# In the first of four batches the chunk of 384 tokens is worked first instead of last

## The chip, the cores and the metric

The kernel runs on one core of a Trainium2 chip. The metric is the device time of one execution in microseconds (us), as a median over executions. The profile is of one execution; its span, from the first to the last instruction, is about 2 us shorter than the device time.

Names used below: TensorE (PE, with its weight loads PEld), VectorE (DVE), ScalarE (ACT), GpSimd (POOL) and SyncE (SP). PSUM is the memory that TensorE writes its products to. A **chunk** is a run of up to 4 tiles of 128 tokens; exT holds the exponentials of the softmax. The **chain** of a page is the work that ended last, followed back from the last instruction to the first; the **granted clock** is the share of full speed that TensorE was given.

## The reference, cut to what matters

```
def _attn_ref(q, k, v, tau):                    # 4 batches, 6016 tokens, 256 channels
    qn = q / (norm(q, axis=1) + 1e-06)
    kn = k / (norm(k, axis=1) + 1e-06)
    s = kn.transpose(0, 2, 1) @ qn / tau        # 256 x 256 for each batch
    ...                                         # softmax of s, row by row: a
    return v @ a
def _moe_ref(x, w_gate, w_val, w_out):          # x: 24064 x 256, weights 256 x 1536
    g = x @ w_gate
    return (silu(g) * (x @ w_val)) @ w_out
```

The kernel multiplies the 256 x 256 softmax into w_gate and w_val for each batch, so the tokens of v go straight through two products with these folded weights (Wg, Wv) and one with w_out. 6016 tokens are 47 tiles: eleven chunks of 4 tiles and an odd one of 3. Since q and k are summed over all tokens and v is handled token by token, the order of v's chunks is free.

## The kernel before

```
chunks = [(s, min(CS, NS - s)) for s in range(0, NS, CS)]     # CS = 4, NS = 47: the 3 come last
...
def load_first_v():
    nc.gpsimd.dma_start(
        out=v0_sb, in_=v[0, :CS * P, :].rearrange("(p s) c -> p s c", s=CS))

def transpose_first_v():                # TensorE, not a transfer: 8 transposes
    vt_ps = psum_o.tile([P, CH, CS * P], BF16, tag="o")
    for h in range(CH):
        for j in range(CS):
            nc.tensor.transpose(vt_ps[:, h, j * P:(j + 1) * P],
                                v0_sb[:, j, h * P:(h + 1) * P], ident)
    ...
def evacuate_first_v(h):
    nc.vector.tensor_copy(vt_ready[(0, 0)][:, h, :], state["vt_ps"][:, h, :])
...
def first_softmax(b):                   # end of the start of batch 0
    ...
    row_eps(rs)
    transpose_first_v()
    keep_warm(2)                        # two products whose result nobody reads
    for h in range(CH):
        evacuate_first_v(h)
    ...                                 # exp -> exT; row sums; first folded weights
    for u in range(4):
        wp_evacuate(b, u, units[u], lo, u % 2 == 1)
    nc.scalar.preload_act_table(ACT.Silu)
...
def gv_matmuls(b, ci, f, between=None): # one of 12 steps f of a chunk
    ...
    for dst, W in ((g_ps, Wg), (v_ps, Wv)):
        if between is not None and dst is v_ps:
            between()                   # in the first chunk: a unit of folded weights
        for kk in range(CH):
            nc.tensor.matmul(dst[:, :mv], W[:, kk, fs], vT[:, kk, :mv],
                             start=(kk == 0), stop=(kk == CH - 1))
...
plan[S1 + 20].append((norm_spread,))    # row of k's norms to all partitions: the tile ink
S2 = S1 + (28 if b == 1 else 34)
plan[S2].append((logits, 0))            # VectorE reads ink, eight steps later
```

Loads go out in the order k, q, v of the first chunk (v0), then the weights, with v of the second chunk among them. Steps 2 to 5 (counted from 0) of the first chunk also compute the other folded weights, whose evacuation out of PSUM alternates between VectorE and ScalarE. The last three lines prepare the next batch while the current one is worked.

## Time and profile before

| | before |
|---|---|
| device time at first, 3 executions | 810.24 us (809.68 to 813.17) |
| span of the profiled execution | 807.6 us |
| TensorE busy | 787.9 us, 98% |
| first value product / second chunk starts | 37.85 / 51.80 us |
| ScalarE's table load | 37.71, for 1.28 us |

To read it: the first 28 us of the chain are loads (of k and q), and nearly all of the rest is TensorE's own work. Around the last softmax step of that start, TensorE, ScalarE, VectorE and the loads hand work to each other within tenths of a microsecond. The lines are in the prediction.

### The profile page before, as it was taken

How to read it: one execution, taken by the hardware profiler on the slowest of the kernel's cores; microseconds unless marked ns; L12 is line 12 of the kernel's file. 1: busy time of each engine (PE TensorE's matmuls, PEld its weight loads, DVE VectorE, ACT ScalarE, POOL GpSimd, SP SyncE). 2: the span in 40 equal slices, each digit the busy share in tenths (PEclk: the TensorE clock that was granted, in tenths of full speed). 3: DMA queues.
4: the chain of work that ended last, by engine and by line, in shares of the span. 5: the costliest groups of instructions: out<-in, count | busy, mean ns of one | idle time of the engine just before them, and what ended most of it. 6: DMA issues, size and time to landing. Idle time of an engine off the chain costs nothing.

```text
span 807.6 us, 11833 instructions
## 1 busy us (share of the span) xinstructions
PE 787.9 (98%) x3867; PEld 384.4 (48%) x3940; DVE 554.7 (69%) x854; ACT 454.3 (56%) x802; POOL 251.0 (31%) x302
## 2 busy tenths in 40 slices
PE   4999999999999999999999999999999999999998
PEld 3644444444454444444454444444445444444446
DVE  4777878758667878766766778766866665665654
ACT  4666666555556666555555656555555555555553
POOL 4415887332104786332000777610000000000000
PEclk8999999999999999999999999999999999999999
DMA  9995999799886685887976697667556665565443
GB/s 89 143 154 97 147 190 174 144 142 178 149 145 144 131 153 121 152 137 166 145 170 144 113 160 149 131 126 166 128 116 123 144 134 131 125 149 130 117 113 99
DMA packets 203567, 112.43 MB, mean 139 GB/s; under 512 B 151424, under 2 KB 190337, under 8 KB 202753
## 3 DMA queue, kind: packets, MB, share of 16 engines
q1 hardware_dynamic: 185456, 84.55, 44.1%
q0 software_dynamic: 17904, 27.01, 30.6%
q8 instruction: 31, 0.51, 0.3%
q14 instruction: 32, 0.25, 0.1%
q10 hardware_dynamic: 144, 0.10, 0.0%
HBM read 79.06 MB, written 60.48 MB: 173 GB/s over the span
## 4 chain that ended last, share of the span: by engine, by line
PE 95%; DMA 3%; issue 1%; ACT 0%; DVE 0%; POOL 0%; ACTq 0%; POOLq 0%
PE g_ps L458 30%; PE v_ps L458 30%; PE o_new L499 29%; PE ps L425 2%; DMA q_sb<-in_q_dram 2%; PE kq_new L171 2%; PE o_new L552 1%; DMA k_sb<-in_k_dram 1%; ACT silu L464 0%; DVE sv L468 0%; PE ss_new L198 0%; PE last_ps L576 0%; PE unit_ps L425 0%; PE kq_new L176 0%; PE ps L415 0%
## 5 line engine op out<-in xcount | busy, mean ns | idle before, releaser
L468 DVE TENSOR_TENSOR sv<-silu,v_ps 128x512 bf16<-128x512 bf16 (+1 forms) x576 | 386.5, 673 | 214.5 <-ACT silu L464 213.1
L464 ACT ACTIVATE silu<-g_ps 128x512 bf16<-128x512 f32 (+1 forms) x576 | 339.1, 589 | 292.5 <-PE g_ps L458 263.7
L458 PE MATMUL g_ps<-vT,Wg 128*128 128x512 bf16 (+1 forms) x1109 | 326.5, 375 | 1.2
L458 PE MATMUL v_ps<-vT,Wv 128*128 128x512 bf16 (+1 forms) x1104 | 325.1, 374 | 1.0
L499 PE MATMUL o_new<-sv,w_out_sb 128*128 128x512 bf16 (+1 forms) x1079 | 319.1, 375 | 1.4
L458 PEld LDWEIGHTS <-Wv 128*128 128x128 bf16 x1152 | 112.7, 98 | 130.9 <-ACT Wv L437 0.4
L303 POOL TENSOR_TENSOR acc_new<-acc_new,sq 128x512 f32<-128x512 f32 x135 | 157.2, 1165 | 52.6 <-DVE sq L293 37.3
L458 PEld LDWEIGHTS <-Wg 128*128 128x128 bf16 x1152 | 111.3, 98 | 125.8 <-DVE Wv L435 0.2
L499 PEld LDWEIGHTS <-w_out_sb 128*128 128x128 bf16 x1104 | 108.0, 98 | 126.5
L129 POOL DMA_DIRECT2D vb_new<-in_v_dram x47 | 24.2, 516 | 244.9 <-DMA vT<-vb_new 243.8
L509 DVE COPY pl<-o_new 128x512 uint16<-128x512 uint16 (+1 forms) x92 | 62.5, 680 | 14.1 <-ACT pl L508 13.9
L293 DVE TENSOR_TENSOR sq<-q_sb 128x512 bf16<-128x512 fp8e5 x72 | 65.8, 914 | 0.0
L508 ACT COPY pl<-o_new 128x512 uint16<-128x512 uint16 (+1 forms) x92 | 53.1, 578 | 19.8 <-PE o_new L499 19.1
L294 ACT ACTIVATE sq<-k_sb 128x512 bf16<-128x512 fp8e5 x72 | 44.2, 614 | 0.0
L171 PE MATMUL kq_new<-k_sb,q_sb 128*128 128x512 fp8e5 x184 | 28.4, 295 | 1.4 <-DMA q_sb<-in_q_dram 1.3
L114 POOL DMA_DIRECT2D q_sb<-in_q_dram x45 | 25.4, 564 | 11.7 <-DMA k_sb<-in_k_dram 9.8
L198 PE MATMUL ss_new<-sq,ones_bf 128*128 128x256 bf16 x83 | 14.8, 336 | 10.9 <-ACT sq L188 10.9
L171 PEld LDWEIGHTS <-q_sb 128*128 128x256 fp8e5 x184 | 21.2, 137 | 6.3 <-DMA q_sb<-in_q_dram 2.7
L114 POOL DMA_DIRECT2D k_sb<-in_k_dram x42 | 23.2, 554 | 2.9 <-DVE sv L468 1.7
L370 POOL TENSOR_SCALAR den<-th 128x512 f32<-128x512 f32 x3 | 1.8, 614 | 64.4 <-ACT th L369 64.4
L338 POOL TENSOR_TENSOR inv<-inv,half 64x8 f32<-64x8 f32 x3 | 5.0, 1665 | 53.3 <-DVE inv L336 53.3
L298 POOL TENSOR_TENSOR acc_new<-sq 128x512 f32<-128x512 bf16 x3 | 3.5, 1151 | 47.1 <-DVE sq L293 47.1
(90 smaller groups left out, 208.4 us busy)
## 6 DMA issues: line engine op xcount, KB each, us to landing
rows<-pl SPq DMA_DIRECT2D x86, 256.0 KB, 2.6
out_dram<-ot_new SPq DMA_DIRECT2D x43, 512.0 KB, 4.1
vb_new<-in_v_dram POOLq DMA_DIRECT2D x43, 256.0 KB, 4.8
q_sb<-in_q_dram POOLq DMA_DIRECT2D x36, 128.0 KB, 5.9
k_sb<-in_k_dram POOLq DMA_DIRECT2D x33, 128.0 KB, 7.4
ot_new<-rows SPq DMA_TRANSPOSE x92, 3.7
k_sb<-in_k_dram POOLq DMA_DIRECT2D x5, 256.0 KB, 9.0
rows<-pl SPq DMA_DIRECT2D x6, 192.0 KB, 2.4
```

The source lines that it names most:

```text
L114: nc.gpsimd.dma_start(out=dst[:, gs:gs + gm, :], in_=src[b].rearrange("(p s) c -> p s c", s=NS)[:, gs:gs + gm, :])
L129: nc.gpsimd.dma_start(out=vb[:mv, :].rearrange("(p s) c -> p (s c)", s=cm), in_=v[b, cs * P:cs * P + mv, :].rearrange("(p s) c -> p (s c)" ...
L171: nc.tensor.matmul(kq[:, jh, :], q_sb[:, ps:ps + 2, js], k_sb[:, ps:ps + 2, :], start=(t == 0 and jh == 0), stop=last, perf_mode=DR, skip_ ...
L293: nc.vector.tensor_mul(sq[:, :pm, 0, :], q_sb[:, ps:ps + pm, :], q_sb[:, ps:ps + pm, :])
L294: nc.scalar.activation(sq[:, :pm, 1, :], k_sb[:, ps:ps + pm, :], ACT.Square)
L303: nc.gpsimd.tensor_tensor(out=acc, in0=acc, in1=sq[:, s, :, :], op=ALU.add)
L458: nc.tensor.matmul(dst[:, :mv], W[:, kk, fs], vT[:, kk, :mv], start=(kk == 0), stop=(kk == CH - 1))
L464: nc.scalar.activation(silu[:, :mv], g_ps[:, :mv], ACT.Silu)
L468: nc.vector.tensor_mul(sv[:, f, :mv], silu[:, :mv], v_ps[:, :mv])
L499: nc.tensor.matmul(self.o_ps[h][:, :self.mv], w_out_sb[:, f, h * P:(h + 1) * P], self.sv[:, f, :self.mv], start=(f == 0), stop=(f == FH - 1))
L508: nc.scalar.copy(pl[:, 0, :self.mv], halves[:, 0, :self.mv])
L509: nc.vector.tensor_copy(pl[:, 1, :self.mv], halves[:, 1, :self.mv])
```

## The change

The intent is plain from the diff: the first chunk's v is the only one that is loaded directly and transposed on TensorE ahead of the first product; three tiles in place of four make that stretch shorter. The odd chunk of batch 0 moves to the front for it.

```diff
-    chunks = [(s, min(CS, NS - s)) for s in range(0, NS, CS)]
-    NCH = len(chunks)
+    odd = NS % CS
+    assert odd
+    plain = [(s, min(CS, NS - s)) for s in range(0, NS, CS)]
+    chunks = [[(0, odd)] + [(s, CS) for s in range(odd, NS, CS)]] + [plain] * (B - 1)
+    NCH = len(plain)
...
-    v0_sb = const.tile([P, CS, C], BF16)
+    v0_sb = const.tile([P, odd, C], BF16)
...
-            out=v0_sb, in_=v[0, :CS * P, :].rearrange("(p s) c -> p s c", s=CS))
+            out=v0_sb, in_=v[0, :odd * P, :].rearrange("(p s) c -> p s c", s=odd))
...
-            for j in range(CS):
+            for j in range(odd):
...
-        nc.vector.tensor_copy(vt_ready[(0, 0)][:, h, :], state["vt_ps"][:, h, :])
+        nc.vector.tensor_copy(vt_ready[(0, 0)][:, h, :odd * P],
+                              state["vt_ps"][:, h, :odd * P])
...   (elsewhere chunks[ci] becomes chunks[b][ci])
```

More of the change, by code (lines that the diff above doesn't have):

```diff
@@ L124, in load_v @@
     def load_v(b, ci):
-        cs, cm = chunks[ci]
+        cs, cm = chunks[b][ci]
         mv = cm * P
@@ L134, in transpose_v @@
     def transpose_v(b, ci):
-        mv = chunks[ci][1] * P
+        mv = chunks[b][ci][1] * P
         vb = vb_loaded.pop((b, ci))
@@ L446, in gv_matmuls @@
     def gv_matmuls(b, ci, f, between=None):
-        cs, cm = chunks[ci]
+        cs, cm = chunks[b][ci]
         mv = cm * P
@@ L470, in out_rows @@
     def out_rows(b, ci):
-        cs, cm = chunks[ci]
+        cs, cm = chunks[b][ci]
         pat = "(p s) c -> p s c" if (b, ci) == (0, 0) else "(s p) c -> p s c"
@@ L483, in __init__ @@
         def __init__(self, b, ci, sv):
-            self.cm = chunks[ci][1]
+            self.cm = chunks[b][ci][1]
             self.mv = self.cm * P
@@ L533, in __init__ @@
         def __init__(self, b, ci, sv):
-            self.cm = chunks[ci][1]
+            self.cm = chunks[b][ci][1]
             self.sv = sv
```

## The prediction

> **What bounds the kernel now.** I read the page's busy times and chain first, to see which engine ends the run.
>
> ```profile
> PE 787.9 (98%) x3867; PEld 384.4 (48%) x3940; DVE 554.7 (69%) x854; ACT 454.3 (56%) x802; POOL 251.0 (31%) x302
> ...
> PE 95%; DMA 3%; issue 1%; ACT 0%; DVE 0%; POOL 0%; ACTq 0%; POOLq 0%
> ```
>
> TensorE is busy 98% of 807.6 us and is 95% of the chain; transfers are 3%, all at the start (loads of k and q, to about 28 us in the chain by time). So a saving counts only if it removes TensorE work or TensorE idle time, or shortens the start. Next I read the timeline of the start, 23 to 52 us, where every edited line runs.
>
> ```profile
> 23.74 0.53 POOL L143 DMA_DIRECT2D v_sb<-in_v_dram  x1 [1.99 <-DMA q_sb<-in_q_dram]
> ...
> 34.93 0.62 PE L150 MATMUL vt_ps<-ident,v_sb 128*128 128x128 bf16 x8
> ...
> 35.33 0.91 ACT L261 ACTIVATE exT<-s_f,inq 128x256 bf16<-128x256 f32 x2 [0.44 <-DVE inq L247]
> ...
> 35.59 0.76 DVE L157 COPY vT_new<-vt_ps 128x512 bf16<-128x512 bf16 x2
> ...
> 35.89 0.11 PEld L267 LDWEIGHTS <-exT 128*128 128x128 bf16 x2 [0.41 <-ACT exT L261]
> ...
> 37.71 1.28 ACT L285 ACT_TABLE_LOAD   x1
> ...
> 39.00 1.08 ACT L464 ACTIVATE silu<-g_ps 128x512 bf16<-128x512 f32 x2
> ...
> 39.65 0.59 PE L458 MATMUL g_ps<-vT_new,Wg 128*128 128x512 bf16 x2
> ...
> 40.15 0.59 PE L425 MATMUL ps<-w_gate_sb,exT 128*128 128x512 bf16 x2
> ...
> 51.80 0.59 PE L458 MATMUL g_ps<-vT,Wg 128*128 128x512 bf16 x2
> ```
>
> The reader is to see four things. The softmax result exT, not v, releases TensorE at 35.89. ScalarE cannot do the first silu before its table load ends at 39.00. The third gate product (39.65) starts about when that first silu ends. The second chunk starts at 51.80. Last I read the transfer views of single issues, for when the data behind v0 arrive (time from issue to landing is the last number).
>
> ```profile
> v_sb<-in_v_dram POOLq DMA_DIRECT2D x1, 256.0 KB, 11.1
> ...
> w_gate_sb<-in_moe_w_gate_dram POOLq DMA_DIRECT2D x1, 256.0 KB, 6.6
> ...
> vT<-vb_new SPq DMA_TRANSPOSE x1, 10.7
> ...
> w_out_sb<-in_moe_w_out_dram POOLq DMA_DIRECT2D x1, 768.0 KB, 14.1
> ```
>
> Issued at 23.74, 33.53, 38.85 and 36.56, they land at about 34.8 (v0), 40.1 (second gate weight piece, used at 40.15), 49.6 (the second chunk's transposed v, used at 51.80) and 50.7 (w_out, first used at 52.67). The margins of the last two are about 2 us each; the first two are just in time.
>
> **What the Trainium skill says.** "TensorE: Matmul & The Clock Gate", section "Back-to-back issue gap", gives a warm gap of N/2.4 + 2.5 ns for one isolated matmul: 215.8 ns at N=512, 162.5 at N=384, and a shorter sustained figure at 512. The trace agrees with the formula: products of 512 columns start 0.216 us apart, and those of 384 at the end 0.163 (two start at 787.08, the next two at 787.41). So 384 tokens cost three quarters; there is no fixed cost to win. "ScalarE: Activation LUTs", section "What ACT_TABLE_LOAD costs", measures 1283 ns and a drain of 1380; the trace has the 1.28 us, and the silu follows at once, with no drain after it. "DMA: Bandwidth & Descriptors", section "Issuing engines are not separate DMA queues", says that all transfers interleave on the same 16 engines. The trace agrees: w_out takes 14.1 us beside the second chunk's transposing transfer.
>
> **Part by part.**
>
> *What is only moved.* Batch 0 has 47 tiles in either order. A chunk of 384 saves 12 x 4 x (0.2158 - 0.163) = 2.5 us of gate and value products, and 24 x 0.053 = 1.3 us of output products, against one of 512. Those 3.8 us now fall in the first two chunks' time and return at the end of batch 0, where a full chunk takes the place of the short one. Balance: zero, if TensorE is saturated at both ends. It is at the old end: around 222 to 246 us the trace has products at 0.216 and 0.163 without gaps, across the boundary of batches too.
>
> *What is removed.* Two of the 8 TensorE transposes go. The 8 take 0.62 us less the pipeline of one (starts from 34.93 to the warming product at 35.39), so some 0.06 each: 0.12 us. But TensorE then waits for exT at 35.89 anyway; the warming products end their issue near 35.82. Worth on the path: 0. The two VectorE copies shrink from 0.76 to about 0.6 us; VectorE then idles 0.24 us for the row sums (36.59) today, so again 0. v0's source shrinks from 512 to 384 KB. The 1 MB loads of k and q each take 2.42 us (issues released at 9.24, 11.70, 14.22, 16.64), so 128 KB is about 0.3 us (an estimate from that rate): everything queued behind v0 lands 0.3 us earlier. The start is q-bound and v0 is behind q, so the start itself does not move, except perhaps 0.07 us where the value weights come just in time (a gap at 36.25).
>
> *What is lost in the first chunk.* The first gate product still starts near 37.4. In the old order TensorE then has g, v (0.86), four short weight products (0.43), g, v (0.86): it reaches the third gate product at 39.6, and the silu that frees its PSUM buffer ends there: a stall of some 0.06. Now it has 0.65 + 0.43 + 0.65 = 1.73 and is there at 39.15. The silu cannot start before 39.00 (the table load is unmoved) and takes about 0.49 at 384 columns (the row at 788.69 shows 0.49), so TensorE starts at about 39.55. New stall 0.4, old 0.06: of the 0.43 saved so far, only 0.1 is kept; **lost: 0.33 us**, or 0.25 if the start gains its 0.07.
>
> *The rest of the chunk.* Four steps with two weight units each cost 4 x 0.163 + 4 x 0.216 = 1.52 us. VectorE has 0.55 + 0.75 = 1.30 in them, ScalarE 0.49 + 0.69 = 1.18, so TensorE still sets the pace; the weight pieces land 0.3 us earlier and TensorE is 0.1 to 0.9 us earlier in them, tight but enough. Six plain steps cost 0.65 each, against ScalarE 0.49 and VectorE 0.55. From 39.55: + 4 x 1.52 + 6 x 0.65 gives 49.5 for the second chunk, 2.3 us before today's 51.80.
>
> *Arrivals there.* The second chunk's v, at 49.6 today, should be there by 49.3 to 49.5; w_out, needed 0.86 us into that chunk at 50.4, lands at about 50.4. Both margins of 2 us are spent almost exactly. I charge **0.1 us** for the two.
>
> *Sum.* 0 (moved work) + 0 (removed) + 0.3 (silu behind the table load) + 0.1 (arrivals) = **+0.4 us**, so 810.24 + 0.4, about 810.6 us.
>
> **The rivals.** (1) *The change pays at the start.* If the transposes waited for v0's landing (34.8, against 34.93 for the first of them), a landing 0.3 us earlier plus 0.12 of transposes would start everything behind it sooner, to 809.8. For it: those two times lie within 0.1 us. Against: TensorE had other work (L389) up to that moment, and the next release is exT at 35.89, which comes from q through ScalarE and not from v0. (2) *The second chunk's v or w_out comes late.* Both transfers are in a stretch where the 16 engines are full to about 48 us, with a sparse tail after. If that tail does not move with v0's 0.3 us, or TensorE gets there sooner than I work out, the stall is 0.3 to 1 us: 811 to 811.5. For it: TensorE needs them 2.3 us sooner and they gain at most 0.3. Against: today's margins are 2 us. (3) *VectorE becomes the bound of the first chunk*, through the two output buffers that its weight evacuations free: 1.30 of 1.52 us a step, worth 0.1 to 0.2 us at the first of them only. (4) *Later background work* (loads of batch 1, norms on GpSimd) runs against a TensorE that is 3.8 us ahead; its steps are counted in chunks, not time, and its margins are many microseconds: 0.
>
> **Range and chances.** My sum has a spread from -0.4 (rival 1) to +1.2 (rival 2), and the three runs before spread from 809.68 to 813.17. So 809.5 to 812.0 should hold it 8 times in 10. Two per cent is 16 us; nothing edited touches more than 5 us of work, and that work is conserved. Faster by 2%: 0.005; within: 0.985; slower: 0.01.
>
> **What would show each step.** Right: exT still released at about 35.9 with 6 transposes ahead of it; the table load still at 37.7; the third gate product at about 39.5 with an idle of some 0.4 us before it; the second chunk's first product between 49.4 and 49.8; products of 512 columns at the end of batch 0; and a total that is flat. Step wrong: if exT comes before 35.8, the start was bound by v0; if the third gate product starts by 39.2, the silu did not hold it; if the second chunk starts after 50, rival 2 holds. The prediction as a whole is wrong if the time falls below 809.5, which needs a saving that I found no place for, or rises over 812, which needs a stall of over 1 us.

## The result, and the profile after

| | before | after |
|---|---|---|
| median of 6 executions | 810.33 us | 810.69 us |
| all six, in order | 809.68, 810.24, 810.29, 810.37, 810.52, 813.17 | 809.90, 810.10, 810.43, 810.95, 811.95, 814.13 |
| ratio of the means | | 1.0007, 95% interval 0.9984 to 1.0029: the same |
| span of the profiled execution | 807.6 us | 812.4 us |

The ratio is the mean time of one kernel's runs over that of the other's of the same rounds, so not quite the ratio of the two medians. Before any line is read, one thing has to be seen: the profiled execution of the changed kernel is the slowest of its six (814.13), and that of before is a quick one (809.42, taken apart from its six and below all of them). **The 4.8 us between the two spans are not the effect of the change**, whose medians differ by 0.36. The work of reading is to find out which parts of the 4.8 belong to the change.

From the page after, busy times and the chain's shares by engine:

```profile
PE 794.6 (98%) x3938; PEld 385.4 (47%) x3938; DVE 554.5 (68%) x854; ACT 454.0 (56%) x802; POOL 250.9 (31%) x302
...
PE 92%; DMA 6%; POOL 1%; issue 0%; DVE 0%; ACT 0%; SPq 0%; POOLq 0%; DVEq 0%; ACTq 0%
```

TensorE still sets the end. The larger busy time is not more work: it is partly matmul records that were missing before (3867 against 3938, though the program has two products fewer), partly slow products. New is that transfers hold 6% of the chain and not 3%.

**The start.** The timeline after; columns are start, length, engine, line, what, count, and in brackets the idle time before and who ended it.

```profile
32.41 0.65 PE L176 MATMUL kq_new<-k_sb,q_sb 128*128 128x512 fp8e5 x4 [1.20 <-DMA q_sb<-in_q_dram]
...
37.06 0.82 PE L154 MATMUL vt_ps<-ident,v_sb 128*128 128x128 bf16 x6
...
37.92 0.62 DVE L161 COPY vT_new<-vt_ps 128x384 bf16<-128x384 bf16 x2 [0.59 <-PE vt_ps L154]
...
38.10 0.15 PEld L272 LDWEIGHTS <-exT 128*128 128x128 bf16 x1 [0.28 <-ACT exT L266]
...
40.65 1.28 ACT L290 ACT_TABLE_LOAD   x1
...
41.63 0.49 PE L463 MATMUL v_ps<-vT_new,Wv 128*128 128x384 bf16 x2
...
41.95 0.49 ACT L469 ACTIVATE silu<-g_ps 128x384 bf16<-128x384 f32 x1
...
43.04 0.49 PE L463 MATMUL g_ps<-vT_new,Wg 128*128 128x384 bf16 x2
```

The matching product of q and k ran at 30.98 before; here its q came late and it ran at 32.41, 1.4 us later, after an idle TensorE. That load was issued at 14.22 in both executions and landed after 18.2 us in place of 16.7. Then the distance grows: the first value product is at 41.63 and not at 37.85, 3.8 us later. The two lines before:

```profile
30.98 0.68 PE L171 MATMUL kq_new<-k_sb,q_sb 128*128 128x512 fp8e5 x4
...
37.85 0.59 PE L458 MATMUL v_ps<-vT_new,Wv 128*128 128x512 bf16 x2
```

The stretches of the trace say why; columns are the stretch, its length, busy time and count for PE, PEld, DVE, ACT and POOL, then the granted TensorE clock, the share of the transfer engines and GB/s. Before:

```profile
33.00:34.00 1.00, 1.00 (x16) 0.74 (x15) 0.70 (x2) 0.98 (x2) 0.96 (x2) 1.00 1.15 194
```

The clock is the third number from the end of the line, here 1.00. After:

```profile
31.00:32.00 1.00, 0.22 (x2) 0.00 (x0) 0.60 (x2) 0.00 (x0) 0.00 (x0) 1.00 1.13 97
32.00:33.00 1.00, 0.59 (x5) 0.42 (x5) 0.54 (x1) 0.53 (x1) 0.35 (x1) 1.00 1.27 159
...
34.00:35.00 1.00, 1.00 (x18) 0.82 (x15) 0.43 (x1) 0.63 (x1) 1.00 (x2) 0.79 1.43 192
35.00:36.00 1.00, 1.00 (x11) 0.70 (x10) 0.00 (x0) 0.00 (x0) 1.00 (x2) 0.50 1.57 222
...
40.00:41.00 1.00, 1.00 (x7) 0.69 (x6) 0.84 (x2) 0.98 (x3) 0.00 (x0) 0.50 1.23 204
41.00:42.00 1.00, 1.00 (x7) 0.62 (x6) 0.93 (x3) 0.99 (x2) 0.00 (x0) 0.80 1.25 206
```

The two thin stretches (TensorE busy 0.22 and 0.59 of 1 us) are followed by 6.8 us at half the clock, from 34.59 to 41.40 (the stretches with 0.79 and 0.80 hold both speeds). The Trainium skill, "TensorE: Matmul & The Clock Gate", section "What's actually happening", states that the clock is full after a busy window and half after an idle one, of about 3.4 us each. The two values agree (1.00 and 0.50), and so does the length: the clock of this trace changes at 14.10, 20.91, 34.59 and 41.40, and the distances of 6.81, 13.68 and 6.81 us are two, four and two times 3.41. But the window did not have to be idle throughout: in the one that ends with the change (31.17 to 34.58) TensorE was busy for 2.21 of 3.41 us, and its longest pause was 1.2. A window with 2.76 us busy (24.69 to 28.10 before, on the same grid counted from that trace's own change at 14.44) was followed by full clock.

Each of the two traces shows one stretch at half clock in its start (14.44 to 21.27 before, 14.10 to 20.91 after); the second one is only in the trace after. The mean granted clocks tell that it belongs to this execution and not to the changed kernel: 0.995 in the trace with one stretch, 0.992 in that with two, and 0.996 to 1.000 in the five other executions of the changed kernel, so at most one in each (an estimate from these means: 6.8 us at half clock lower the mean of 810 us by 0.004). That the late q comes of the change is neither shown nor likely: the load stands ahead of v0 in the queue, and the kernel before also has one execution of 813.17 us among six, of which no trace was kept.

**The first chunk.** From the first value product to the second chunk it takes 53.35 - 41.63 = 11.72 us after, and 51.80 - 37.85 = 13.95 before: 2.23 us shorter. The 46 gate and value products in that stretch are 0.0533 us shorter each, 2.45 in all. So 0.22 us are lost. After:

```profile
49.34 0.69 ACT L442 ACTIVATE Wv<-ps,smr 128x512 bf16<-128x512 f32 x1 [0.45 <-PE ps L430]
...
49.93 0.88 ACT L469 ACTIVATE silu<-g_ps 128x384 bf16<-128x384 f32 x2
...
50.44 1.02 DVE L473 TENSOR_TENSOR sv<-silu,v_ps 128x384 bf16<-128x384 bf16 x2 [0.64 <-ACT silu L469]
50.46 0.48 PE L463 MATMUL g_ps<-vT_new,Wg 128*128 128x384 bf16 x2
...
51.05 0.49 PE L463 MATMUL v_ps<-vT_new,Wv 128*128 128x384 bf16 x2
...
53.35 0.59 PE L463 MATMUL g_ps<-vT,Wg 128*128 128x512 bf16 x2
```

Two products of 384 columns start 0.33 us apart; here 0.59 us lie between 50.46 and 51.05. The value product waited for a PSUM buffer that VectorE frees (read from the order, as the profile names no releaser there: the kernel has two such buffers, and the product at 50.44, of some 0.55 us, leaves one near 50.99); VectorE waited for the silu; and the silu came behind ScalarE's last weight evacuation (0.69 us at 49.34). That is 0.26 of the idle time; with gaps of 0.03 at three other places it makes 0.35, against 0.13 in the kernel before (0.06 ahead of 39.65, 0.07 ahead of 40.15), and the difference is the 0.22. Before, the same hand-over was just in time: VectorE's product at 48.03, of 0.69 us, left the buffer near 48.72, and the value product came at 48.78 without a gap:

```profile
46.83 0.69 ACT L437 ACTIVATE Wv<-ps,smr 128x512 bf16<-128x512 f32 x1 [0.55 <-PE ps L425]
...
48.03 1.40 DVE L468 TENSOR_TENSOR sv<-silu,v_ps 128x512 bf16<-128x512 bf16 x2 [0.72 <-ACT silu L464]
...
48.78 0.59 PE L458 MATMUL v_ps<-vT_new,Wv 128*128 128x512 bf16 x2
```

**Single issues after**, with the time from issue to landing last:

```profile
v_sb<-in_v_dram POOLq DMA_DIRECT2D x1, 192.0 KB, 11.2
...
w_gate_sb<-in_moe_w_gate_dram POOLq DMA_DIRECT2D x1, 256.0 KB, 6.3
...
w_out_sb<-in_moe_w_out_dram POOLq DMA_DIRECT2D x1, 768.0 KB, 12.9
...
vT<-vb_new SPq DMA_TRANSPOSE x1, 9.1
```

Issued at 23.73, 33.92, 36.72 and 38.95, they land at 34.9, 40.2, 49.6 and 48.1. The last q landed at 34.0 (33.6 before), so v0 needed 0.9 us behind it and not 1.2: the smaller load is worth its 0.3 us, which the late q took away again. The second chunk's v is there 1.5 us sooner than before and nothing waited for it.

**Later in batch 0** the new share of transfers in the chain shows up. The chain in order of time, after:

```profile
169.50 3.80 DMA row<-inv
...
173.76 14.29 DMA ink<-row
...
188.14 0.06 DVE s_new L366
...
188.54 0.69 DVE sv L473
...
189.28 0.59 PE v_ps L463 x2
```

and the timeline at the same place:

```profile
188.14 0.48 DVE L366 SCALAR_TENSOR_TENSOR s_new<-kq_new,inq,ink 128x256 f32<-128x256 f32 x1 [1.89 <-DMA ink<-row]
...
189.28 0.59 PE L463 MATMUL v_ps<-vT,Wv 128*128 128x512 bf16 x2 [0.49 <-DVE sv L473]
```

The row of k's norms for the next batch, spread to all partitions, took 14.3 us to land; before, 10.2:

```profile
ink<-row SPq DMA_DIRECT2D x1, 128.0 KB, 10.2
...
185.91 0.48 DVE L361 SCALAR_TENSOR_TENSOR s_new<-kq_new,inq,ink 128x256 f32<-128x256 f32 x1
...
188.36 0.59 PE L458 MATMUL v_ps<-vT,Wv 128*128 128x512 bf16 x2
```

Before, it landed about 183.8 and was read at 185.91, with 2.1 us to spare and no wait. After, VectorE stood still for 1.89 us, did its products of silu and value late, and TensorE lost time too: the same value product is 188.36 before and 189.28 after, 0.92 later, where the two kernels had been 0.26 apart at the last group of products of q and k (144.12 and 144.38). So this wait cost 0.66 us.

**The account of the 4.8 us**, from those landmarks (the two lines with 0.0533 are computed from the change in length of one product):

| piece | us |
|---|---|
| late q and half clock, up to the first value product (41.63 - 37.85) | +3.78 |
| first chunk, from there to the second (11.72 - 13.95) | -2.23 |
| output products of the first chunk, 24 x 0.0533 | -1.28 |
| wait for the spread norms | +0.66 |
| a full chunk in place of the short one at the end of batch 0, 72 x 0.0533 | +3.84 |
| sum | +4.77 |
| measured at the short chunk of batch 1 (414.15 - 409.40) | +4.75 |

The distance stays at 4.75 to the end (the last products start at 807.49 and 802.74). The sum closes, and so it does at the landmarks between (0.27 computed and 0.26 measured at 144, 0.93 and 0.92 at 189), so nothing else of size happens. The first pair of gate products lies ahead of the first landmark; its two shorter products (0.1 us) are inside the 3.78. Moved work comes out even, as 2.45 + 0.1 + 1.28 against 3.84. **What the change itself can have cost in this execution is the 0.22 us in the first chunk**, and 0.66 us more if the late norms are its doing.

### The profile page after: what moved, and what is told of

It reads as the page before. It is cut to its first block, busy times and chain, and to the rows that moved or that the text cites. A ratio compares the mean times of both kernels' runs of the same rounds, so it can differ in the third digit from the quotient of the medians.

```text
span 812.4 us, 11902 instructions
## 1 busy us (share of the span) xinstructions
PE 794.6 (98%) x3938; PEld 385.4 (47%) x3938; DVE 554.5 (68%) x854; ACT 454.0 (56%) x802; POOL 250.9 (31%) x302
## 3 DMA queue, kind: packets, MB, share of 16 engines
q1 hardware_dynamic: 185840, 84.62, 45.5%
## 4 chain that ended last, share of the span: by engine, by line
PE 92%; DMA 6%; POOL 1%; issue 0%; DVE 0%; ACT 0%; SPq 0%; POOLq 0%; DVEq 0%; ACTq 0%
PE v_ps L463 29%; PE g_ps L463 29%; PE o_new L504 28%; PE ps L430 2%; DMA q_sb<-in_q_dram 2%; PE kq_new L176 2%; DMA ink<-row 2%; DMA k_sb<-in_k_dram 1%; PE o_new L557 1%; DMA row<-inv 0%; DVE sv L473 0%; PE ps L420 0%; PE unit_ps L430 0%; POOL k_sb L118 0%; POOL inv L343 0%
## 5 line engine op out<-in xcount | busy, mean ns | idle before, releaser
L463 PE MATMUL v_ps<-vT,Wv 128*128 128x512 bf16 (+1 forms) x1128 | 331.9, 376 | 0.5 <-DVE sv L473 0.5
L463 PE MATMUL g_ps<-vT,Wg 128*128 128x512 bf16 (+1 forms) x1128 | 332.1, 376 | 0.0
L504 PE MATMUL o_new<-sv,w_out_sb 128*128 128x512 bf16 (+1 forms) x1104 | 324.7, 376 | 0.0
```

Source lines behind the costliest of these rows:

```text
L463: nc.tensor.matmul(dst[:, :mv], W[:, kk, fs], vT[:, kk, :mv], start=(kk == 0), stop=(kk == CH - 1))
L504: nc.tensor.matmul(self.o_ps[h][:, :self.mv], w_out_sb[:, f, h * P:(h + 1) * P], self.sv[:, f, :self.mv], start=(f == 0), stop=(f == FH - 1))
```

## The experiments

**No experiment gave a result.** Four kernels were first sent with q and k multiplied as before, in the matmul mode DoubleRow; kernels with that mode were held back at that time and were not run. They were then rewritten without it and sent in 20 more submissions, over some three and a half hours; no chip ran any of them. What follows is therefore the plan with its expectations, not evidence. All four share this edit, which lengthens the kernel but is not meant to touch the first chunk's steps:

```diff
-            if pm == 2:
-                nc.tensor.matmul(kq[:, jh, :], q_sb[:, ps:ps + 2, js],
-                                 k_sb[:, ps:ps + 2, :],
-                                 start=(t == 0 and jh == 0), stop=last,
-                                 perf_mode=DR, skip_group_check=True)
...
+            for s in range(pm):
+                nc.tensor.matmul(kq[:, jh, :], q_sb[:, ps + s, js], k_sb[:, ps + s, :],
+                                 start=(t == 0 and jh == 0 and s == 0),
+                                 stop=last and s == pm - 1, skip_group_check=True)
```

**The base.** The kernel before with that edit alone.

> The base for the other runs: the kernel before, with each DoubleRow product of two tiles of q and k written as two plain products (that matmul mode could not be run in the experiments). Every theory: right result; some 8 products of 0.132 us per group become 16 of 0.108, 0.67 us for each of 18 groups of the later batches, so 12 us longer, about 822 us; the start, which is bound by the loads of q, 0.1 to 0.3 us later. The first chunk (first gate product to the second chunk) still 14.4 us.

Measured: nothing. It was to carry the comparison of the others, and to give a second trace of the old start.

**The changed kernel in a second execution**, with the same edit.

> The changed kernel with each DoubleRow product of two tiles of q and k written as two plain products (that matmul mode could not be run in the experiments). Every theory: right result; 8 products of 0.132 us per group become 16 of 0.108, 0.67 us for each of 18 groups of the later batches, so some 12 us longer than the changed kernel. What is looked at is its start, in an execution without the late load of q. My theory: exT releases TensorE near 36; the third gate product is held some 0.4 us behind the silu, which waits for the table load; one more wait of 0.3 us where the weight evacuations end; the first chunk (first gate product to the second chunk) takes 12.0 to 12.4 us against 14.4, where the removed columns alone are 2.5. Rival, v0 bounds the start: the first gate product comes 0.2 to 0.4 us after v0 and not after exT. Rival, late arrivals: the second chunk's first product waits for the transposed v. Rival, late norms (the profiled execution of the changed kernel had one): the spread row of k's norms lands after VectorE needs it in batch 0, TensorE idle 0.5 us or more near 190.

Measured: nothing. It was the most wanted run: the one trace of the changed kernel has the disturbed start, so what an undisturbed start does at the third gate product was not seen.

**A double dose**: a first chunk of 2 tiles, to make a loss in the first chunk large enough for the clock.

```diff
-    chunks = [[(0, odd)] + [(s, CS) for s in range(odd, NS, CS)]] + [plain] * (B - 1)
+    first = [2] + [CS] * 10 + [3, 2]
+    chunks = [[(sum(first[:i]), n) for i, n in enumerate(first)]] + [plain] * (B - 1)
+    odd = first[0]
...   (the list and the buffers of v's chunks count 13 in batch 0)
```

> A double dose, plain products: batch 0 in 13 chunks, the first of 2 tiles, then ten of 4, then 3 and 2. My theory: what does not shrink with the tokens (table load 1.28, weight evacuations, arrival of the second chunk's v) holds the first chunk, so of the 5.2 us of products that leave it only some 2.6 are gained: 2 to 3.5 us slower than the control of 13 chunks. TensorE shows idle time before the third gate product (about 0.7), in the steps with weight evacuations, and before the second chunk (1 to 2). Rival, v0 bounds the start: v0 lands 0.6 us sooner and 4 transposes fewer: 0.5 to 0.8 us faster than the control.

Measured: nothing.

**Its control**: the same number of chunks with a first one of 4 tiles.

```diff
+    first = [CS] * 10 + [3, 2, 2]
...   (all else as in the double dose)
```

> The control for the double dose, plain products: batch 0 in 13 chunks, ten of 4 tiles, then 3, 2 and 2; the first chunk as in the kernel before. My theory: products cost by their columns alone, so 13 chunks in place of 12 cost nothing: within 0.5 us of the base with plain products. A fixed cost of a product or of a chunk would show as 1 us or more.

Measured: nothing. So everything below rests on one trace of each kernel and twelve times.

## Why the prediction was right or wrong

The time was foretold as 810.6 us and was 810.69, inside 809.5 to 812.0, and the class (the same) is right. But a difference of 0.36 us between medians, with an interval of about 0.2% either way, can't tell +0.4 from 0 or from -1. That the forecast and the median agree to 0.1 us is luck, and the total is no proof of the sum's terms. By its steps:

**Moved work balances: borne out.** The trace after has products at 0.216 and 0.163 us as foretold, and the distance between the two traces grows from 0.92 us (at 189) to 4.75 by the end of batch 0 and stays there: 3.83 measured, where 3.84 were to return. This is why a quarter less work in the first chunk is worth nothing: TensorE is just as full where the tokens went.

**The removed transposes and copies are off the path: consistent, not proved.** After, 6 transposes stood ahead of exT, and exT released TensorE (0.28 us of idle before the weight load at 38.10). The v0 load had landed 2.1 us before the first transpose (34.9 against 37.06). But in that execution everything behind q was late, so this says nothing of a start in which v0 and the transposes fall within 0.1 us of each other. Rival 1 is weakened only by the medians: a gain of 0.4 us was not seen, but the interval (some -1.3 to +2.3 us) does not exclude it. One thing the prediction left out: the work of the two transposes goes to the transfers, as all but three tiles of batch 0 now take the transposing one, where all but four did. Queue q1 moved 84.62 MB and not 84.55, the 64 KB of one tile; no cost of it is seen.

**v0's 0.3 us: right in size, worth nothing.** 0.9 us behind the last q and not 1.2. The gate and value weights that follow landed within 0.2 us of the old times, because q itself was 0.4 later.

**The silu behind the table load, +0.33: not seen.** This was the largest term of the sum. After, the table load ended at 41.93, the silu that frees the buffer ran from 41.95 to 42.44, and the third gate product started at 43.04, directly behind the value product of 42.72: no wait, and 0.6 us to spare. The reason is in the clock: at half speed the last folded weights took so long that ScalarE was ahead. Its table load began 0.55 us before the first gate product (40.65 and 41.20), and before the change some 0.3 us after it (37.71, with the product near 37.42). Whether the wait exists at full clock stays open; the working for it is untouched, but no trace shows it.

**The rest of the first chunk: pace right, end missed.** Steps with weights were foretold at 1.52 us and took (49.14 - 43.04)/4 = 1.525. For the plain steps I compared each engine's busy time per step with TensorE's and found room. I didn't follow the hand-over: ScalarE's last evacuation of 0.69 us stands ahead of a silu, and with steps of 0.65 us there is no longer a slack to absorb it. It cost 0.26 us. Busy time per step tells whether an engine can keep up on average, not whether one long instruction in its queue is late once.

**Arrivals, +0.1: not there.** The second chunk's v landed 9.1 us after its issue and not 10.7, and w_out 12.9 and not 14.1; nothing waited. I had moved their landings by v0's 0.3 us alone. That w_out took 14.1 us beside the transposing transfer fits with transfers that interleave, but one duration doesn't prove it.

**Later background work, 0: wrong in this execution.** I wrote that its margins are many microseconds. The margin of the spread norms was 2.1 us, to be read from the trace of before (landing 10.2 after an issue at 173.6, use at 185.91), and I had not looked. The wait was 0.66 us. Whether the change causes it is open. For it: from the second chunk on, the changed order sits elsewhere against the transfers. Against: eight steps lie between issue and use in both kernels, none of them shortened there, and the issue times of the two executions are 0.2 us apart (173.6 and 173.8); the fastest two executions of the changed kernel (809.90 and 810.10) are below the median of before, which leaves little room for 0.66 us in each. Two more things in the traces speak for chance. The loads that GpSimd issues just before are the same, 0.26 us apart (169.18 to 171.86 before, 169.44 to 172.12 after). And in the next two batches, whose work the change does not touch, the landing time of this transfer also differs between the two executions (8.8 and 9.3 us, 3.3 and 5.0), though by less than these 4.1. I take it for chance in the transfers, argued and not shown.

So the number was right while the sum behind it was right in its large part (balance, nothing gained at the start) and, for the small rest, not the sum that the trace has: 0.33 + 0.1 was foretold, and 0.22 at another place, with perhaps 0.66 at a third, was found.

## What to carry to other kernels

Before work is moved out of a stretch because that stretch comes early, look at whether the engine that sets the end is full where the work goes: then only the idle time counts, and shorter steps can add some by exposing fixed pieces (an evacuation, a table load) that longer steps had covered. When two profiled executions differ by more than the medians do, subtract landmark by landmark before reading a cause into the difference. The margin of each background transfer is worth one line of reading (landing against first use), even when the change doesn't touch it.

## What the Trainium skill lacked or had wrong

- "TensorE: Matmul & The Clock Gate", "What's actually happening": half clock is said to follow an idle window of about 3.4 us. The length is borne out (changes of the clock are whole multiples of 3.41 us apart), but here it followed a window in which TensorE was busy for 2.21 of 3.41 us, with no pause over 1.2. The page has no figure for a window that is partly busy; here half clock followed 2.21 us of busy time and full clock 2.76, in one case each.
- The same page, "Back-to-back issue gap": its sustained 131 ns for 512 columns isn't seen; the products of this kernel run for 750 us at 216 ns, its formula for one isolated product, which also holds at 384 columns (0.163 us).
- "ScalarE: Activation LUTs", "What ACT_TABLE_LOAD costs": the load is 1.28 us as stated, but the drain of 1.38 isn't in either trace; the load starts 0.02 us after the work ahead of it, and the silu 0.01 to 0.02 us after the load.
- No page gives what a small spread of one row to all partitions takes while transposing transfers run: 10.2 and 14.3 us from issue to landing in two executions; the second made VectorE wait for 1.89 us, its longest wait for a transfer after the start.
